# Masking a top-k attention row with its threshold as the bias

## The chip, the cores and the metric

The kernel runs on one core of a Trainium2 chip. The metric is the device time of one execution in microseconds. Five engines of the core work side by side, each through its own queue, in order: TensorE (PE in the profile; its weight loads are PEld), VectorE (DVE), ScalarE (ACT), GpSimd (POOL) and SyncE (SP), which issues most of the transfers here. An engine waits for another by semaphores.

## What is computed

Two blocks in a row: attention in which each query keeps only its 32 best keys, then a two-layer network with ELU between the layers. 8 batches, 8 heads, 576 positions, 64 per head; then 4608 tokens of 512, widened to 2048. Cut to what matters:

```python
scores = scale * np.matmul(q, k.transpose(0, 1, 3, 2))
kth = np.partition(scores, -32, axis=-1)[..., -32:-31]     # the threshold
scores = np.where(scores >= kth, scores, -1000000000.0)
scores = scores - np.max(scores, axis=-1, keepdims=True)
attn = np.exp(scores)
attn = attn / (np.sum(attn, axis=-1, keepdims=True) + 1e-09)
x = np.matmul(attn, v)            # then heads are put side by side: (4608, 512)
h = x @ w_in
g = np.where(h > 0.0, h, np.exp(np.minimum(h, 0.0)) - 1.0)
out = g @ w_out
```

## The kernel before

**Steps.** The attention is cut into 144 steps. A step is up to 128 queries of a pair of heads, so it has two score tiles of 128 queries by 576 keys, numbered i = 0 and 1. For each step these things happen, spread over several rounds of the main loop so that the engines overlap:

- `scores` (L299, L307): TensorE multiplies queries and keys, ScalarE copies the result out of PSUM into the tile `sc`. This runs two steps ahead.
- `select` (L341, L346, L353), or `select_row` in the first eight steps (L318, L322, L328): VectorE finds the 32 largest of each row, eight at a time. A maximum instruction gives the eight largest, a match-and-replace takes them out, and so on four times. The first eight stay in `u.first`, whose first column is the largest of the row. The last eight stay in `u.last`, whose eighth column is the threshold.
- `mask` (L366 to L370), once for each of the two tiles: two small GpSimd instructions form `neg` (minus the threshold) and `gap` (threshold minus largest), then two ScalarE activations over the whole tile, in place: a leaky ReLU with a slope of 1e30 on the negative side, and the exponential with the row sum as a second output. The first leaves the kept scores as score minus threshold and throws the others far below zero. The second adds `gap`, so that the kept ones become score minus largest, and the others give zero.
- `normalise` (L380 to L387): GpSimd forms the reciprocal of the row sums in small instructions and multiplies both tiles by it.
- `turn` (L406, L407): TensorE transposes the tile, ScalarE copies it to `et`.
- `attend` (L432, L459): TensorE multiplies with v, ScalarE copies the result to `xT`.

The network works on blocks of tokens as they become complete: `hidden` (L504 on TensorE; L514, L517 and L519 on ScalarE; the closing gate L476 on VectorE) and `project` (L529, L538). `feed` hands out these pieces between the attention's parts, paced by a list of due times.

**Weights.** The weights come in as 64-bit words and are turned into fp32 on the chip. Each of 32 pieces takes three ScalarE activations (L174, L175, L178), one GpSimd instruction (L179), one VectorE instruction (L186) and one more on GpSimd (L187). All ScalarE parts are issued from within `select_row` in the first eight steps, two pieces for each score tile, ahead of that tile's `mask`.

**Order.** From step 8 on (`tight`) the instructions of TensorE, ScalarE, VectorE and GpSimd stand in their queues as the program lists them. The opening lines and the first eight steps differ: the opening is in manual order too, but steps 0 to 7 are outside it, and the framework's planner, which walks through a model of the program by priority and readiness, decides the order in each queue. In these steps `mask` is called for the step in hand, right after the selection of each tile:

```python
                next(passes)
                mask(cur, i)
                feed(n, 0.25)
```

From step 8 on it is called one round later, for the step before: `mask(prev, 0)` after the first maxima of the step in hand, `mask(prev, 1)` two passes later, then `normalise(prev)` at the end of the round. Step 7 was already masked, and is skipped there.

The small tiles (`neg`, `gap`, `den`, the rows of eight) come from a pool with four buffers for each name.

Of the kernel before, what the change touches and what calls it, by code (L numbers as in the profile page):

```python
# [8 lines left out]
AF = mybir.ActivationFunctionType  # L9
ALU = mybir.AluOpType  # L10
FP32 = mybir.dt.float32
# [5 lines left out]
TOP_K = 32  # L17
TAKEN = -1.0e30
EPS = 1.0e-9
STEEP = 1.0e30  # L20
HIDDEN = {1: 1.1, 2: 1.85, 3: 2.7}
PROJECT = 3.55

# [58 lines left out]
def kernel(  # L82
# [9 lines left out]
    nc = tc.nc  # L92
    P = nc.NUM_PARTITIONS
# [12 lines left out]
    scale = 1.0 / float(D) ** 0.5  # L106
# [3 lines left out]
    def pool(name, bufs, **kw):  # L110
        return ctx.enter_context(tc.tile_pool(name=name, bufs=bufs, **kw))
# [7 lines left out]
    small = pool("small", 4)  # L119
# [161 lines left out]
    def turn_qk(whole=False):  # L281
        while turning:
            if next(turning[0], turning) is turning:
                turning.pop(0)
            elif not whole:
                return
# [3 lines left out]
    def scores(u):  # L290

        u.sc = scpool.tile([P, 2, S], FP32, tag="sc", name="sc")
        q0 = QUERIES + u.t.qt * P
        for half in range(2):
            for h, i, rows in u.heads:
                kq = kqT[u.t.b, h // 2]
                part = slice(i * D, (i + 1) * D)
                k0 = (KEYS if i == 0 else 0) + half * HS
                nc.tensor.matmul(  # L299
                    wide[i][rows, half, 0:HS],  # L300
                    kq[part, q0 : q0 + u.t.ql],
                    kq[part, k0 : k0 + HS],
                    start=True,
                    stop=True,
                )
        for i in range(2):
            nc.scalar.activation(  # L307
                u.sc[:, i, :].rearrange("p (a s) -> p a s", a=2),
                wide[i][:, :, 0:HS], AF.Copy, scale=scale,
            )  # L310

    def select_row(u, i):
        if i == 0:
            u.first = small.tile([P, 2, 8], FP32, tag="m1", name="m1")
            u.last = small.tile([P, 2, 8], FP32, tag="m4", name="m4")
        sc = u.sc[:, i, :]
        m = u.first[:, i, :]
        nc.vector.max(m, sc)  # L318
        wk = wkpool.tile([P, S], FP32, tag=f"wk{i}", name="wk")
        cur = sc  # L320
        for r in range(TOP_K // 8 - 1):
            nc.vector.match_replace(wk[:], m, cur, TAKEN)  # L322
            cur = wk[:]
            if r < TOP_K // 8 - 2:
                m = small.tile([P, 8], FP32, tag=f"m{i}", name="m")[:]
            else:
                m = u.last[:, i, :]
            nc.vector.max(m, cur)  # L328
            if r > 0:
                hook()  # L330
            if r != 1:
                yield
# [21 lines left out]
            hook()  # L354
            yield

    def mask(u, i):

        if u.masked:
            return  # L360
        if i == 0:
            u.den = small.tile([P, 2], FP32, tag="den", name="den")
        u.masked = i == 1
        sc, low, top = u.sc[:, i, :], u.last[:, i, 7:8], u.first[:, i, 0:1]
        neg = small.tile([P, 1], FP32, tag="neg", name="neg")
        nc.gpsimd.tensor_scalar_mul(neg[:], low, -1.0)  # L366
        gap = small.tile([P, 1], FP32, tag="gap", name="gap")
        nc.gpsimd.tensor_tensor(gap[:], low, top, ALU.subtract)
        nc.scalar.activation(sc, sc, AF.Prelu, bias=neg[:], alpha=STEEP)  # L369
        nc.scalar.activation(  # L370
            sc, sc, AF.Exp, bias=gap[:], accum_out=u.den[:, i : i + 1]
        )

    def normalise(u):

        if u.normal:
            return
        u.normal = True
        den = small.tile([P, 2], FP32, tag="dene", name="dene")
        nc.gpsimd.tensor_scalar_add(den[:], u.den[:], EPS)  # L380
        rec = small.tile([P, 2], FP32, tag="rec", name="rec")
        nc.gpsimd.tensor_tensor(rec[:], den[:], power[:], ALU.pow)
        nc.gpsimd.tensor_tensor(den[:], den[:], rec[:], ALU.mult)
        nc.gpsimd.tensor_scalar(den[:], den[:], -1.0, 2.0, ALU.mult, ALU.add)
        nc.gpsimd.tensor_tensor(rec[:], rec[:], den[:], ALU.mult)
        for i in range(2):
            nc.gpsimd.tensor_scalar(  # L387
                u.sc[:, i, :], u.sc[:, i, :], rec[:, i : i + 1], 1.0, ALU.mult, ALU.mult
            )
# [26 lines left out]
    def attend(g):  # L416
        t = g.tiles[0]
        ps = ps_t.tile([P, JP], FP32, tag="t", name="avps")
        n = P if t.rem else sum(x.ql for x in g.tiles)
        for k in range(2 if t.rem else 1):  # L420
            hp = 2 * g.hp + k if t.rem else g.hp
            vt = vT[t.b, hp]
            for c in range(J + 1):
                for i in range(2):
                    chunk = J if c == J else i * (J + 1) + c
                    w = g.et[:, chunk, :, :].rearrange("p a q -> p (a q)")
                    cols = slice(0, n)
                    if t.rem:
                        c0 = R * (k if i == 0 else 1 - k)
                        w = w[:, c0 : c0 + R]  # L430
                        cols = slice(k * R, (k + 1) * R)
                    nc.tensor.matmul(  # L432
                        ps[i * D : (i + 1) * D, cols],
                        vt[:, 2 * J + i if c == J else i * J + c, :],
                        w,
                        start=(c == 0),
                        stop=(c == J),
                    )
        if t.rem:
            finish(t.block, 2, slice(2 * g.hp, 2 * g.hp + 2), t.cols,  # L440
                   ps[:, 0:n].rearrange("p (a q) -> p a q", a=2))
            return
        c0 = 0
        tiles = list(g.tiles)
        while tiles:
            blk, lo, parts = tiles[0].block, tiles[0].cols.start, 0
            while tiles and tiles[0].block is blk:
                parts += 1
                hi = tiles.pop(0).cols.stop
            finish(blk, parts, g.hp, slice(lo, hi), ps[:, c0 : c0 + hi - lo])  # L450
            c0 += hi - lo
# [201 lines left out]
    def step(n):  # L653
        return steps[n] if 0 <= n < NS else None
# [3 lines left out]
    for n in range(NS + 3):  # L658
        for fn, args in todo.pop(n, []):
            fn(*args)  # L660
        ahead, cur, prev, done = step(n + 2), step(n), step(n - 1), step(n - 2)
        if n < tight:
            turn_qk(True)
            scores(ahead)
            for i in range(2):
                passes = select_row(cur, i)
                next(passes)
                if i == 0:
                    while closing:
                        attend(closing.pop(0))  # L670
                elif prev:
                    normalise(prev)
                    turn(prev, main)
                    turn(prev, rest)
                    turn(prev, other)
                feed(n, 0.25)
                next(passes)
                mask(cur, i)
                feed(n, 0.25)
            continue  # L680
        if n == tight:
            ctx.enter_context(tc.manual_schedule(engines=engines))
        passes = select(cur) if cur else iter(range(4))
        if ahead:
            scores(ahead)
        while closing:
            attend(closing.pop(0))
        next(passes)
        feed(n, 0.25)
        if prev:  # L690
            mask(prev, 0)
        turn_qk()
        next(passes)
        feed(n, 0.25)
        if done:
            turn(done, main)
            turn(done, rest)
        if prev:
            mask(prev, 1)
        next(passes)  # L700
        feed(n, 0.25)
        if done:
            turn(done, other)
        next(passes)
        if prev:
            normalise(prev)
        feed(n, 0.25)
        turn_qk(True)
# [36 lines left out]
```

## Time and profile before

| | |
|---|---|
| runs | 1666.01, 1667.40, 1667.79 us; median 1667.4 |
| profiled execution | 1667.02 us, its span 1665.2 us |
| instructions | 25986 |
| TensorE busy | 1592.8 us (96%) |
| VectorE busy | 1495.8 us (90%) |
| ScalarE busy | 1165.1 us (70%) |
| GpSimd busy | 630.5 us (38%) |
| granted TensorE clock, mean | 0.977 |

The span runs from the first to the last instruction of the profiled execution; 1.8 us of its time lie outside it. A line of the profile names the source line, the engine, the operation, the tiles written and read (out<-in) and their shapes. A group's line then gives the number of instructions, the busy time in us, the mean duration in ns, and the idle time of the engine just ahead of them with what ended it. A waits line gives total us, number of times and the longest. A timeline line starts with the start in us and the duration. The duration covers an instruction's whole record, and on VectorE and ScalarE records of neighbours overlap, so the next one can start before the printed end. The lines by stage give busy us and, in brackets, the number of instructions for each engine; then the granted clock, the share of the transfer engines in use, and GB/s.

### The profile page before, as it was taken

Reading aid. Unit: us, or ns where it says so; the run is one execution under the profiler, and the core shown is the slowest. Engines: PE = TensorE matmul, PEld = TensorE weight load, DVE = VectorE, ACT = ScalarE, POOL = GpSimd, SP = SyncE. Lnnn points to the kernel's source line nnn. Section 1 sums busy time; section 2 is a strip of 40 time slices with the busy share of each in tenths; the row PEclk is TensorE's granted clock in tenths of the full one; section 3 lists DMA queues with packets and bytes.
Section 4 is the critical chain, followed back from the end, with each engine's and each line's share of the span. In section 5 each row is a group of like instructions: output and inputs, shape, how many; then the busy total and the mean of one; then the engine's idle time right before and its main releaser. Section 6 shows DMA issues by size and latency. Waiting matters only on the chain.

```text
span 1665.2 us, 25986 instructions
## 1 busy us (share of the span) xinstructions
PE 1592.8 (96%) x8528; PEld 1031.5 (62%) x8528; DVE 1495.8 (90%) x3044; ACT 1165.1 (70%) x2377; POOL 630.5 (38%) x1719
## 2 busy tenths in 40 slices
PE   5589999999999999999999999999999999999999
PEld 3366677657574767656566676755557575755565
DVE  5887999999999999999999999999999999998500
ACT  6998777668686777678667685868758585857521
POOL 3775444333334334333334333333333343332200
PEclk9578999999999999999999999999999999999999
DMA  7540120001100110001100111001200100000000
GB/s 211 171 144 7 23 50 29 7 15 44 48 1 8 43 42 22 1 28 37 42 14 1 50 29 35 1 14 43 50 13 1 28 15 29 7 7 7 7 13 13
DMA packets 101126, 56.21 MB, mean 34 GB/s; under 512 B 84096, under 2 KB 92288, under 8 KB 100992
## 3 DMA queue, kind: packets, MB, share of 16 engines
q1 hardware_dynamic: 99792, 54.26, 11.7%
q8 instruction: 68, 1.11, 0.3%
q14 instruction: 66, 0.54, 0.1%
q10 hardware_dynamic: 1200, 0.30, 0.1%
HBM read 45.09 MB, written 9.44 MB: 33 GB/s over the span
## 4 chain that ended last, share of the span: by engine, by line
PE 65%; DVE 21%; ACT 9%; POOL 3%; issue 2%; SPq 0%; DMA 0%; ACTq 0%; POOLq 0%; DVEq 0%
PE ops L529 24%; PE hps L504 20%; DVE wk L346 9%; DVE m L353 8%; PE avps L432 7%; PE scps L299 6%; PE eps L406 5%; DVE m L341 3%; ACT sc L370 2%; ACT sc L369 1%; DVE gT L476 1%; ACT raw L175 1%; PE qkps L269 1%; ACT et L407 1%; POOL w_in L187 1%
## 5 line engine op out<-in xcount | busy, mean ns | idle before, releaser
L353 DVE MAX8 m<-wk 128x8 f32<-128x576 f32 x816 | 577.0, 750 | 0.0
L504 PE MATMUL hps<-xT,w_in 128*128 128x256 f32 (+2 forms) x2432 | 548.1, 374 | 12.5 <-ACT xT L459 12.3
L529 PE MATMUL ops<-w_out,gT 128*128 128x512 f32 x1152 | 522.8, 598 | 0.0
L504 PEld LDWEIGHTS hps<-xT,w_in 128*128 128x128 f32 x2432 | 406.5, 193 | 109.2 <-issue 23.8
L346 DVE MATCH_REPLACE8 wk<-m,wk 128x576 f32<-128x576 f32 x544 | 400.8, 746 | 0.0
L529 PEld LDWEIGHTS ops<-w_out,gT 128*128 128x128 f32 x1152 | 208.7, 190 | 233.0 <-issue 219.5
L380 POOL TENSOR_SCALAR dene<-den 128x2 f32<-128x2 f32 x144 | 35.9, 249 | 771.2 <-ACT sc L370 770.6
L369 ACT ACTIVATE sc<-sc,neg 128x576 f32<-128x576 f32 x288 | 226.8, 788 | 89.2 <-POOL neg L366 89.0
L370 ACT ACTIVATE sc<-sc,gap 128x576 f32<-128x576 f32 x288 | 224.1, 778 | 25.7 <-ACT sc L369 0.7
L387 POOL TENSOR_SCALAR sc<-sc,rec 128x576 f32<-128x576 f32 x288 | 221.0, 778 | 14.9
L307 ACT ACTIVATE sc<-scps 128x576 f32<-128x576 f32 x288 | 174.0, 659 | 73.3 <-PE scps L299 73.3
L299 PE MATMUL scps<-kqT 64*128 64x288 f32 (+1 forms) x1280 | 201.8, 440 | 21.2 <-ACT kqT L275 7.9
L407 ACT COPY et<-eps 128x512 f32<-128x512 f32 x288 | 166.8, 579 | 55.2 <-PE eps L406 55.0
L346 DVE MATCH_REPLACE8 wk<-m,sc 128x576 f32<-128x576 f32 x272 | 200.4, 746 | 0.0
L432 PE MATMUL avps<-et,vT 128*64 128x256 f32 (+2 forms) x2080 | 193.3, 326 | 4.8 <-ACT et L407 4.6
L406 PEld LDWEIGHTS eps<-ident,sc 128*128 128x128 f32 x1152 | 143.6, 144 | 83.8 <-issue 46.2
L476 DVE SCALAR_TENSOR_TENSOR gT<-n,gT 128x512 f32<-128x512 f32 (+1 forms) x132 | 100.2, 759 | 102.0 <-ACT n L519 101.9
L341 DVE MAX8 m<-sc 128x8 f32<-128x576 f32 x272 | 191.8, 748 | 0.0
L406 PE MATMUL eps<-ident,sc 128*128 128x128 f32 x1152 | 175.7, 278 | 15.4 <-POOL sc L387 13.0
L432 PEld LDWEIGHTS avps<-et,vT 128*64 128x64 f32 x2080 | 122.6, 141 | 79.1 <-issue 22.8
L299 PEld LDWEIGHTS scps<-kqT 64*128 64x128 f32 (+1 forms) x1280 | 108.1, 181 | 91.9 <-issue 44.2
L514 ACT ACTIVATE n<-hps 128x512 f32<-128x512 f32 (+1 forms) x156 | 88.0, 564 | 71.4 <-PE hps L504 67.5
(47 smaller groups left out, 1170.2 us busy)
## 6 DMA issues: line engine op xcount, KB each, us to landing
kin<-in_k_dram SPq DMA_DIRECT2D x64, 128.0 KB, 2.8
raw<-in_moe_w_in_dram SPq DMA_DIRECT2D x16, 512.0 KB, 5.4
vT<-in_v_dram SPq DMA_DIRECT2D x64, 128.0 KB, 2.3
raw<-in_moe_w_out_dram SPq DMA_DIRECT2D x16, 512.0 KB, 3.9
out_dram<-osb SPq DMA_DIRECT2D x32, 256.0 KB, 2.3
qin<-in_q_dram SPq DMA_DIRECT2D x62, 128.0 KB, 2.8
kin<-in_k_dram SPq DMA_DIRECT2D x32, 32.0 KB, 2.4
vT<-in_v_dram SPq DMA_DIRECT2D x64, 16.0 KB, 2.2
```

The source lines that it names most:

```text
L299: nc.tensor.matmul(wide[i][rows, half, 0:HS], kq[part, q0 : q0 + u.t.ql], kq[part, k0 : k0 + HS], start=True, stop=True,)
L341: nc.vector.max(found[i], cur[i])
L346: nc.vector.match_replace(wk[i], found[i], cur[i], TAKEN)
L353: nc.vector.max(found[i], cur[i])
L369: nc.scalar.activation(sc, sc, AF.Prelu, bias=neg[:], alpha=STEEP)
L370: nc.scalar.activation(sc, sc, AF.Exp, bias=gap[:], accum_out=u.den[:, i : i + 1])
L387: nc.gpsimd.tensor_scalar(u.sc[:, i, :], u.sc[:, i, :], rec[:, i : i + 1], 1.0, ALU.mult, ALU.mult)
L406: nc.tensor.transpose(ps[:, c * P : (c + 1) * P], sc[:, c0 : c0 + P], ident[:])
L407: nc.scalar.copy(g.et[:, chunks, u.at, :], ps[:, 0 : n * P].rearrange("p (c q) -> p c q", c=n),)
L432: nc.tensor.matmul(ps[i * D : (i + 1) * D, cols], vt[:, 2 * J + i if c == J else i * J + c, :], w, start=(c == 0), stop=(c == J),)
L504: nc.tensor.matmul(blk.h[:, f % bank, :], w_in[:, i, f * P : (f + 1) * P], blk.xT[:, i, 0:n_tok], start=(i == 0), stop=(i == NC - 1),)
L529: nc.tensor.matmul(blk.o[:], blk.gT[f // NG][:, f % NG, s * P : (s + 1) * P], w_out[:, f, :], start=(f == 0), stop=(f == NF - 1),)
```

## The change

The leaky ReLU is given the difference the other way round: threshold minus score, which it forms with a scale of -1 and the threshold itself as the bias. The scores below the threshold are then the positive ones and pass as they are; the kept ones are negative and are made small by a slope of 2 to the power -96. The exponential multiplies by minus 2 to the power 96, which brings the kept ones back to score minus threshold and throws the others far below zero, and adds `gap` as before. `neg` is not needed any more. The constant becomes a power of two. The engine that forms `gap` is now an argument of `mask`: GpSimd by default, VectorE where `mask` is called in the first eight steps.

```diff
-STEEP = 1.0e30
+STEEP = 2.0**96
...
-    def mask(u, i):
+    def mask(u, i, engine=nc.gpsimd):
...
         sc, low, top = u.sc[:, i, :], u.last[:, i, 7:8], u.first[:, i, 0:1]
-        neg = small.tile([P, 1], FP32, tag="neg", name="neg")
-        nc.gpsimd.tensor_scalar_mul(neg[:], low, -1.0)
         gap = small.tile([P, 1], FP32, tag="gap", name="gap")
-        nc.gpsimd.tensor_tensor(gap[:], low, top, ALU.subtract)
-        nc.scalar.activation(sc, sc, AF.Prelu, bias=neg[:], alpha=STEEP)
+        engine.tensor_tensor(gap[:], low, top, ALU.subtract)
+        nc.scalar.activation(sc, sc, AF.Prelu, scale=-1.0, bias=low, alpha=1.0 / STEEP)
         nc.scalar.activation(
-            sc, sc, AF.Exp, bias=gap[:], accum_out=u.den[:, i : i + 1]
+            sc, sc, AF.Exp, scale=-STEEP, bias=gap[:], accum_out=u.den[:, i : i + 1]
         )
...
-                mask(cur, i)
+                mask(cur, i, nc.vector)
```

## The prediction

> **What bounds the kernel now.** I read the page first (VectorE 90% busy, TensorE 96%), then the busy time of each engine by stage, because shares over the whole span mix stages with different limits.
>
> ```profile
> core 0: us, PE busy (x) PEld busy (x) DVE busy (x) ACT busy (x) POOL busy (x), PEclk, DMA share, GB/s
> ...
> 36.00:58.00 22.00, 6.46 (x43) 4.93 (x43) 15.02 (x31) 21.27 (x34) 13.26 (x24) 0.65 0.59 203
> 58.00:139.00 81.00, 63.22 (x320) 46.88 (x320) 59.74 (x122) 79.72 (x139) 58.50 (x98) 0.67 0.42 129
> ...
> 146.00:850.00 704.00, 688.16 (x4018) 453.97 (x4017) 704.00 (x1441) 506.01 (x1060) 275.54 (x793) 1.00 0.10 27
> 850.00:1550.00 700.00, 697.55 (x3670) 444.40 (x3669) 668.93 (x1355) 496.19 (x1030) 258.46 (x739) 1.00 0.07 20
> 1550.00:1606.00 56.00, 55.75 (x187) 27.46 (x186) 15.66 (x32) 18.36 (x39) 10.36 (x29) 1.00 0.04 10
> ```
>
> The reader is to see three limits, one after the other. From 36 to about 145 us (steps 0 to 7, with the weight conversion) ScalarE is full: 21.27 + 79.72 of 103 us, so 2.0 us are idle. From 146 to 850 VectorE is busy in all 704 us. From 850 to the end TensorE is: 697.55 of 700. A microsecond saved counts only where it lies on the full engine of its stage.
>
> Next I read the groups with shapes kept apart, for the masking instructions and for two that show what an immediate costs.
>
> ```profile
> L369 ACT ACTIVATE sc<-sc,neg 128x576 f32<-128x576 f32 x288 | 226.8, 788 | 89.2 <-POOL neg L366 89.0
> L370 ACT ACTIVATE sc<-sc,gap 128x576 f32<-128x576 f32 x288 | 224.1, 778 | 25.7 <-ACT sc L369 0.7
> ...
> L366 POOL TENSOR_SCALAR neg<-m 128x1 f32<-128x1 f32 x288 | 74.1, 257 | 74.3 <-DVE m L353 63.1 <-DVE m L328 10.7
> ...
> L514 ACT ACTIVATE n<-hps 128x512 f32<-128x512 f32 x108 | 64.5, 597 | 43.8 <-PE hps L504 42.5
> L517 ACT ACTIVATE gT<-hps 128x512 f32<-128x512 f32 x108 | 64.5, 597 | 0.0
> ...
> L368 POOL TENSOR_TENSOR gap<-m,m 128x1 f32<-128x1 f32 x288 | 56.0, 194 | 0.1
> ```
>
> The tempting number is the 89.0 us that ScalarE sat idle until `neg` was there. The view of the waits, cut by stage, says where: 60.0 us (39 times) between 146 and 850, 25.7 (32 times) between 850 and 1550, 3.3 (once) after that; together 89.0. None is left for the first 146 us. What ScalarE waited for between 36 and 146 us is only this:
>
> ```profile
> ACT et L407 <- PE eps L406: 2.0, 3, 0.7
> ACT et L407 <- PE scps L406: 0.2, 1, 0.2
> ```
>
> The timeline of GpSimd ahead of one of those three waits, then ScalarE's own:
>
> ```profile
> 64.43 0.21 POOL L366 TENSOR_SCALAR neg<-m 128x1 f32<-128x1 f32 x1 [2.41 <-DVE m L328]
> 64.60 0.19 POOL L368 TENSOR_TENSOR gap<-m,m 128x1 f32<-128x1 f32 x1
> 64.88 1.61 POOL L179 TENSOR_SCALAR raw<-raw 128x512 f32<-128x512 f32 x2
> 66.57 2.30 POOL L187 TENSOR_TENSOR w_in<-raw 128x512 int32<-128x512 int32 x2
> 68.96 0.23 POOL L380 TENSOR_SCALAR dene<-den 128x2 f32<-128x2 f32 x1
> ...
> 70.92 1.48 POOL L387 TENSOR_SCALAR sc<-sc,rec 128x576 f32<-128x576 f32 x2
> ```
>
> ```profile
> 71.42 0.80 ACT L369 ACTIVATE sc<-sc,neg 128x576 f32<-128x576 f32 x1
> 72.88 0.58 ACT L407 COPY et<-eps 128x512 f32<-128x512 f32 x1 [0.65 <-PE eps L406]
> ```
>
> GpSimd works in order: `neg` held it for 2.41 us, with weight conversion and normalisation queued behind. ScalarE later waits 0.65 us for a transpose that waited for that normalisation.
>
> **`neg` goes (288 instructions on GpSimd).** In steps 8 to 143 the first activation is released by VectorE's maximum directly. Worked on one step: the maximum's record ends near 503.7 us, `neg` starts at 503.76, the activation at 504.02, so about 0.26 us sooner. At most 72 waits of 0.26 us = 19 us of ScalarE idleness go; the rest of the 89 us is waiting for VectorE itself. Up to 850 us VectorE has no idle time to give back: 0. What was late next is VectorE's maximum. From 850 on TensorE would have to wait for ScalarE to gain, and its whole idle time there is 2.4 us, put down mostly to scores copies and transposed keys, not to masks: I take 0, bounds -2.4 and 0. If these covers were gone, 19 us would be the price. Where GpSimd was behind with a normalisation (near 153 us, a wait of 2.48 us), the first activation starts early but the second still needs `gap` from the same queue.
>
> **`gap` on VectorE (16 instructions, steps 0 to 7).** No such VectorE instruction is in the trace. The nearest small one is the value load of 128x8 (L346, mean 82 ns; the next instruction starts 0.07 us after it): 16 x 0.07 = 1.1 us. The Trainium skill, page "VectorE: DVE Perf Modes", section "Side-by-side: where the cycles go for N=2048 bf16", gives every instruction some 150 cycles of start-up at 0.96 GHz, an estimate of 0.16 us, or 16 x 0.16 = 2.5 us. I take the trace's 1.1 us and keep 2.5 as the end. Either is covered between 36 and 139 us, where VectorE is busy 74.76 of 103 us (28 us idle). Only three masks fall into 16 to 36 us, where VectorE is nearly full: 0.2 to 0.5 us, were they on the path. Below zero is excluded on VectorE itself. `gap` waits for nothing there, both inputs being VectorE's own, except a free buffer (four): at the sixteenth mask that means the exponential of the twelfth, which ended at 112.1 us, 11 us before `gap` can start. Behind it in VectorE's queue stand selection and conversion.
>
> **GpSimd relieved (32 instructions in steps 0 to 7).** 16 x (0.26 + 0.19) = 7.2 us less, and no stop at `neg`. At 64 us: the first L178 ends at 63.77, so L179 could start at 63.85, 1.03 us before 64.88. L187 and normalisation follow about 1 us sooner, the transpose with them, and the 0.65 us wait goes. The other two waits (0.70 at 57.2 us, 0.63 at 87.2) have the same queue ahead of them. Sum 0.70 + 0.65 + 0.63 = 2.0 us on the engine that is full to 146 us. A rule speaks against part of it: "GPSIMD Engine Reference", section "Specifications", says that GpSimd contends with VectorE instructions that have two SBUF inputs, and `gap` has two. The trace shows that contention: a `neg` at 504.43 us took 0.57 us beside the two-input L476, against a median of 220 ns. By the rule up to 16 x 0.16 = 2.5 us return to GpSimd of 7.2 taken off; by the trace's duration 1.1. The 1 us lead at each wait survives both.
>
> **The turned signs.** L514 (scale -1) and L517 (none) both take 597 ns, so a scale as an immediate costs nothing. Both activations keep one bias column. A bias read from the eighth column of a row, instead of from a tile of its own, has no row of its own; I take 0. As a bound, L369's mean and median differ by 7 ns (788, 781), and 16 masks of that are 0.1 us, either sign.
>
> **The sum.** 2.0 saved, 0 in the steady steps, 0 for VectorE. Against the profiled execution (span 1665.2, time 1667.02): 1665.0. The median of the runs is 0.4 above: 1665.4.
>
> **The rivals.** Steps 0 to 7 are not in the manual order; the framework places their instructions, and the trace shows that it does move them: step 8's first maximum (L341) ran at 120.56 us, before step 7's L328 at 122.54.
>
> *A new order at the start.* ScalarE was idle from 24.3 to 26.69 us, and the first threshold was there at 25.96 (a maximum's record of 0.75 us from 25.21), but the two L369 of step 0 stand behind two L307 and one L275, at 28.23. With no `neg` to wait for they may be placed first. Then they start near 26.0 and the chain mask, normalisation, transpose, conversion comes 2.0 us sooner. The delayed L307 are not needed until VectorE's L318 at 35.84. For it: an idle engine. Against: the placed order may stay as it was. Time: 1665.4 - 2.0 = 1663.4.
>
> *A worse order at the hand-over.* VectorE's steady run begins at 139.14 us, after a gate (L476, 138.53) that waited 3.42 us for the exponential L519. On ScalarE that L519 (137.69) stands just ahead of a pair of conversions; such a pair takes 4.65 us (66.91 to 71.56). If the removal and the added VectorE instruction let the planner place one more pair ahead of L519, everything after starts 4.65 us later. The 2.0 us hang on the same order, so I count them as lost with it: 1667.4 + 4.65 = 1672.0 (1670.0 if they survive). One displaced pair decides it. For it: the planner sees other ready times. Against: ScalarE was 19 us behind `neg` at the sixteenth mask (123.39 to 142.73), so `neg` did not decide its order. The mirror case, a pair moved behind, gives 1660.8, with the first rival 1658.8.
>
> *It does nothing.* The three waits close for another reason: 1667.4.
>
> **How the numbers follow.** About 0.2% (3.3 us) is what a measurement of this kernel tells from no change: faster means below 1664.1, slower above 1670.7. The forecast, with the case of nothing, 0.50; the better orders 0.31, all but 0.01 beyond the bound; a worse one 0.19, of which 0.02 for the milder 1670.0, so 0.17 beyond the bound. That gives faster 0.30, same 0.53, slower 0.17. The range 1659 to 1672 reaches to the mirror case and to one pair lost.
>
> **What would show it.** L366 is gone, and 16 small VectorE instructions appear. Waits of ScalarE for L366 turn into waits for VectorE's maxima. The first L346 starts near 137 us instead of 139.14. VectorE stays full for the 700 us after it and TensorE to the end, both stages as long as before. The forecast is wrong if the steady stages change their length, if the start moves by over 4 us, or if ScalarE gets idle time in the first 145 us.

## The result and the profile after

| | before | after |
|---|---|---|
| median of the runs | 1667.59 us (20 runs, 1665.69 to 1669.1) | 1664.1 us (20 runs, 1663.01 to 1665.44) |
| profiled execution, its span | 1667.02, 1665.2 us | 1665.44, 1663.6 us |
| GpSimd busy | 630.5 us | 570.3 us |
| VectorE busy | 1495.8 us | 1498.0 us |

The ratio is 0.9981, with a 95% interval of 0.9975 to 0.9987. That is 3.2 us less, between 2.2 and 4.2: a small gain, but a real one. (The two medians themselves lie 3.5 us apart.) The forecast was 1665.4, 2.0 us below the median of 1667.4 that it started from. The profiled execution of the changed kernel is the highest of its 20 runs, so the difference of the two spans, 1.6 us, is too small a reading of the gain; why it came out so high is told under before_again.

The busy time by stage of the changed kernel, with the columns and the stages as in the prediction:

```profile
36.00:58.00 22.00, 6.99 (x43) 5.09 (x42) 15.53 (x35) 20.82 (x34) 11.66 (x17) 0.66 0.53 188
58.00:139.00 81.00, 64.23 (x332) 47.97 (x332) 63.61 (x136) 81.00 (x141) 55.60 (x78) 0.67 0.42 133
...
146.00:850.00 704.00, 688.44 (x4019) 455.01 (x4018) 704.00 (x1440) 507.43 (x1063) 248.41 (x654) 1.00 0.10 27
850.00:1550.00 700.00, 697.55 (x3671) 444.31 (x3670) 668.39 (x1357) 494.63 (x1029) 231.59 (x609) 1.00 0.07 20
```

ScalarE is now busy in all 81.00 us from 58 to 139, where 1.28 us were idle before. From 36 to 58 it is idle for 1.18 us, where it was 0.73. The other two limits stand: VectorE 704.00 of 704, TensorE 697.55 of 700. GpSimd has lost 27 us in each of these two stages, and no other engine there moved by as much as 2 us.

The groups that mask, with shapes kept apart (busy us, mean ns; then the idle time ahead of them and what ended it):

```profile
L372 ACT ACTIVATE sc<-sc,m 128x576 f32<-128x576 f32 x288 | 228.2, 793 | 48.9 <-DVE m L353 48.7
L373 ACT ACTIVATE sc<-sc,gap 128x576 f32<-128x576 f32 x288 | 225.0, 781 | 38.5 <-POOL gap L371 15.2 <-ACT sc L372 0.4
...
L371 POOL TENSOR_TENSOR gap<-m,m 128x1 f32<-128x1 f32 x272 | 56.1, 221 | 91.2 <-DVE m L353 91.2
...
L371 DVE TENSOR_TENSOR gap<-m,m 128x1 f32<-128x1 f32 x16 | 5.0, 312 | 0.0
```

`neg` is gone. The leaky ReLU is released by VectorE's maximum itself, and the exponential waits 15.2 us for `gap`, which is now the first GpSimd instruction behind that maximum. ScalarE's idle time ahead of the two activations was 89.2 + 25.7 = 114.9 us and is 48.9 + 38.5 = 87.4: 27.5 us are gone. The kernel gained 3.2. Nearly all of these 27.5 lay beside full engines, as the prediction had it. What ScalarE still waits for between 36 and 146 us, from the view of the waits:

```profile
ACT sc L307 <- PE scps L299: 0.9, 1, 0.9
ACT et L410 <- PE scps L409: 0.2, 1, 0.2
```

The three waits for transposed tiles (0.70, 0.65, 0.63) are gone; one for scores is new. The place shown in the prediction, on the timelines of GpSimd and of ScalarE in the changed kernel:

```profile
64.47 1.61 POOL L179 TENSOR_SCALAR raw<-raw 128x512 f32<-128x512 f32 x2 [2.44 <-ACT raw L178]
66.16 1.04 POOL L187 TENSOR_TENSOR w_in<-raw 128x512 int32<-128x512 int32 x1
...
68.68 0.22 POOL L383 TENSOR_SCALAR dene<-den 128x2 f32<-128x2 f32 x1
...
70.63 1.48 POOL L390 TENSOR_SCALAR sc<-sc,rec 128x576 f32<-128x576 f32 x2
```

```profile
63.63 1.29 ACT L178 ACTIVATE raw<-raw 128x512 f32<-128x512 f32 x2
...
71.94 0.82 ACT L372 ACTIVATE sc<-sc,m 128x576 f32<-128x576 f32 x1
72.60 0.63 ACT L410 COPY et<-eps 128x512 f32<-128x512 f32 x1
```

GpSimd's stop is now ended by L178, not by a maximum. The first L178 ends at 63.63 + 0.65 = 64.28 and L179 starts at 64.47, 0.19 us behind it; before it was 1.11 us behind. (The row of two L178 is 1.29 us long; one takes 0.65.) So the lead gained is 0.92 us (1.03 forecast), and the copy L410 carries no bracket any more: it waits for nothing.

### The profile page after: what moved, and what is told of

The parts are those of the page before. It is cut to its first block, busy times and chain, and to the rows that moved or that the text cites. A ratio compares the mean times of both kernels' runs of the same rounds, so it can differ in the third digit from the quotient of the medians.

```text
span 1663.6 us, 25707 instructions
## 1 busy us (share of the span) xinstructions
PE 1592.8 (96%) x8528; PEld 1032.3 (62%) x8528; DVE 1498.0 (90%) x3060; ACT 1163.5 (70%) x2377; POOL 570.3 (34%) x1415
## 3 DMA queue, kind: packets, MB, share of 16 engines
q8 instruction: 68, 1.11, 0.3%
## 4 chain that ended last, share of the span: by engine, by line
PE 57%; DVE 32%; ACT 7%; issue 2%; POOL 1%; SPq 0%; DMA 0%; ACTq 0%; DVEq 0%; POOLq 0%
PE ops L532 21%; PE hps L507 18%; DVE wk L346 14%; DVE m L353 12%; PE avps L435 6%; PE scps L299 6%; PE eps L409 4%; DVE m L341 4%; DVE gT L479 2%; ACT raw L175 2%; ACT sc L373 1%; PE qkps L269 1%; ACT sc L372 1%; ACT raw L174 1%; ACT raw L178 1%
## 5 line engine op out<-in xcount | busy, mean ns | idle before, releaser
L346 DVE MATCH_REPLACE8 wk<-m,wk 128x576 f32<-128x576 f32 x544 | 398.7, 738 | 0.0
L372 ACT ACTIVATE sc<-sc,m 128x576 f32<-128x576 f32 x288 | 228.2, 793 | 48.9 <-DVE m L353 48.7
L373 ACT ACTIVATE sc<-sc,gap 128x576 f32<-128x576 f32 x288 | 225.0, 781 | 38.5 <-POOL gap L371 15.2
L410 ACT COPY et<-eps 128x512 f32<-128x512 f32 x288 | 167.6, 582 | 66.8 <-PE eps L409 66.6
L346 DVE MATCH_REPLACE8 wk<-m,sc 128x576 f32<-128x576 f32 x272 | 199.3, 738 | 0.0
```

The source lines that it names most:

```text
L346: nc.vector.match_replace(wk[i], found[i], cur[i], TAKEN)
L372: nc.scalar.activation(sc, sc, AF.Prelu, scale=-1.0, bias=low, alpha=1.0 / STEEP)
L373: nc.scalar.activation(sc, sc, AF.Exp, scale=-STEEP, bias=gap[:], accum_out=u.den[:, i : i + 1])
```

## One table for all kernels

Each trace can be cut at two instants that all kernels have. The first is the start of the fourth activation of L174 (at 36.67 us before), where ScalarE's full stretch with the weight conversion begins. The second is the start of the first L346 of step 8, where VectorE's full stretch begins. "Start" is the time up to the first, "conversion" the time from the first to the second, "steady" the rest of the span. "Behind L175" is the part of the conversion behind the start of the tenth L175 (at 54.16 us before). From there to the second instant ScalarE has the same instructions in the same order in all kernels; ahead of it the last four rows differ. These four times come from the profiled execution; median, range and ratio to before come from the timed runs (7 to 20 of each kernel, 5 or 6 where a star stands). Each ratio is to runs of before that were taken along with the kernel, with medians of 1667.42 to 1667.59.

| kernel | start | conversion | behind L175 | steady | median (range) | ratio [95%] |
|---|---|---|---|---|---|---|
| before | 36.67 | 102.48 | 84.98 | 1526.10 | 1667.59 (1665.69 to 1669.1) | 1 |
| before_again | 35.36 | 102.47 | 84.99 | 1526.09 | 1667.16 (1665.71 to 1669.02) | 0.9997 [0.9988, 1.0006] |
| after | 36.95 | 101.26 | 82.85 | 1525.43 | 1664.1 (1663.01 to 1665.44) | 0.9981 [0.9975, 0.9987] |
| again_after | 35.77 | 100.91 | 82.78 | 1525.21 | 1664.61 (1662.99 to 1665.62) | 0.998 [0.9972, 0.9989] |
| new_early | 36.94 | 101.02 | 83.55 | 1526.68 | 1665.8 (1664.55 to 1666.41) | 0.9987 [0.9978, 0.9995] |
| new_late | 37.07 | 103.78 | 85.38 | 1525.16 | 1666.43 (1664.99 to 1668.21) | 0.9994 [0.9985, 1.0003] |
| gap_gpsimd | 35.75 | 102.37 | 84.49 | 1525.46 | 1665.37 (1663.82 to 1666.99) | 0.9988 [0.998, 0.9997] |
| idle_neg | 36.09 | 100.79 | 82.71 | 1525.38 | 1664.05 (1663.28 to 1664.96) | 0.9978 [0.9969, 0.9987] |
| no_gap_late | 35.94 | 100.87 | 82.70 | 1524.38 | 1662.89 (1662.19 to 1664.32) | 0.9972 [0.9961, 0.9983] |
| gap_vector_all* | 37.79 | 101.06 | 82.74 | 1534.62 | 1674.83 (1672.71 to 1675.29) | 1.0039 [1.0027, 1.0052] |
| old_vector_early | 35.30 | 102.30 | 83.27 | 1526.32 | 1664.37 (1663.74 to 1665.7) | 0.9981 [0.9972, 0.999] |
| mix | 35.24 | 102.40 | 83.38 | 1525.39 | 1663.98 (1662.71 to 1664.85) | 0.9978 [0.9969, 0.9987] |
| mix_no_gap* | 34.81 | 102.30 | 83.26 | 1524.27 | 1663.21 (1661.88 to 1663.73) | 0.9971 [0.9959, 0.9982] |
| no_gap_all* | 35.40 | 100.52 | 82.25 | 1524.24 | 1662.76 (1661.94 to 1663.83) | 0.9971 [0.9959, 0.9982] |

Two things are to be read from it. "Start" scatters by over 1 us between executions of one program, while "conversion" and "steady" of one program repeat to 0.01 us (before) or 0.35 and 0.22 us (after). And "steady" falls into groups. The six kernels that turn the signs from step 8 on and form `gap` on GpSimd there have 1525.16 to 1525.46; the four with the old masking there have 1526.09 to 1526.68. The groups stand apart, but a difference of 0.5 us within a group is no effect: new_early, whose steps from 8 on are those of before, has 1526.68.

## The experiments

**before_again: how far two executions of one program differ.** No edit.

> The kernel before against itself: ratio 1.000, within 0.5 us. For the second profile: the stretch from the first L346 to the end repeats to 0.3 us (1526.1), while the first L346 may lie anywhere from 138 to 141 us, since new_late, whose start is the same program, had 140.85. If instead the stretch moves by more than 0.5 us, the 0.9 us read from it for the steps after 8 is not safe.

Conversion and steady stretch came out equal to 0.01 us, but the start was 1.31 us shorter. The difference is there at 24 us. One row of TensorE's timeline, of before and then of before_again:

```profile
24.37 2.29 PE L299 MATMUL scps<-kqT 64*128 64x288 f32 x8 [0.75 <-ACT kqT L265]
```

```profile
24.21 1.24 PE L299 MATMUL scps<-kqT 64*128 64x288 f32 x8 [0.75 <-ACT kqT L265]
```

The same eight matmuls took 2.29 us in one execution and 1.24 in the other, with a granted clock of 1.00 in both from 24 to 27 us; why, no run here shows. The profile of after drew the long start too: 36.95, and a clock of 0.50 from 34 to 38 us, where before had 0.77 and before_again 0.98. With 1.18 us less of it, as in again_after, it would lie near the middle of its runs instead of at their top.

**again_after: the changed kernel once more.** No edit.

> The changed kernel once more, for a second profile. Theory A (the gain is GpSimd's relief in the first eight steps, passed on by a full ScalarE): the first L346 starts 1 to 2.5 us before the 139.14 us of before (the first profile of the changed kernel had 138.21, with the granted TensorE clock at 0.50 between 34 and 38 us where before had 0.77), and the time is 2 to 4 us below before. Theory B (the gain is made after step 8, by the 288 waits that lose neg): the hand-over differs by under 1 us and the rest of the gain grows between 146 and 1600 us. Theory C (fewer GpSimd instructions beside VectorE's two-input gate L479): the gates in 146 to 850 us lose up to 1.4 us of extra time against before.

The median was 1664.61. Conversion and steady stretch were short again: 1.57 and 0.89 us below before, against 1.22 and 0.67 in the first profile. The steady stretch was forecast to stay as it was, and did not.

**new_early and new_late: each half of the change alone.** In the first, steps 0 to 7 have the new masking and the later ones the old, with the edit below. In the second it is the other way round: its condition reads `if engine is nc.vector:`.

```diff
     def mask(u, i, engine=nc.gpsimd):
...
+        if engine is nc.gpsimd:
+            neg = small.tile([P, 1], FP32, tag="neg", name="neg")
+            nc.gpsimd.tensor_scalar_mul(neg[:], low, -1.0)
...
+            nc.scalar.activation(sc, sc, AF.Prelu, bias=neg[:], alpha=STEEP)
...
+            return
```

> Turned subtraction and gap on VectorE in steps 0 to 7 only; from step 8 on neg, gap and the old subtraction as before. Theory A: the whole gain, 2 to 3.5 us below before. Theory B: at most 1 us below before. Theory C: as A for its part before 146 us, so 1 to 2 us below before.

> The old masking in steps 0 to 7, the turned one (gap on GpSimd) from step 8 on. Theory A: no change, within 0.7 us of before. Theory B: nearly the whole gain, 2 to 3.5 us below before. Theory C: 0.3 to 1.4 us below before, with the gates in 146 to 850 us shorter by that much.

The table takes the halves apart. new_early has the short conversion (101.02) and the old steady stretch (1526.68). new_late has the short steady stretch (1525.16), and its conversion is not short (103.78). It is even 1.3 us longer than before, through a wait of 0.89 us for scores and one of 0.32 for a transposed tile that before did not have. Its instructions in these steps are those of before, so this is scatter: its granted clock was 0.50 from 34 to 38 us, as in the profile of after, which has the same wait for scores. By the medians new_early is 1.6 us under before and new_late 1.0; the interval of new_late includes no change. So the change gains in two places, where the prediction had one.

**gap_gpsimd: is it the move of `gap` to VectorE, or the turned signs, that clears the start?**

```diff
-                mask(cur, i, nc.vector)
+                mask(cur, i)
```

> The changed kernel with gap on GpSimd in the first eight steps too, so neg alone is gone there and gap still waits for VectorE in GpSimd's queue. Theory A, where the stop at VectorE's maximum counts: gap takes over neg's stop (2.41 us before the one at 64.43 us), only 16 x 0.26 us of work go, and half the gain or less is left, 0.5 to 1.5 us below before. If only the number of GpSimd instructions counted: two thirds of the gain, about 2.3 us. Theory B: the same time as the changed kernel.

The conversion is back at 102.37. GpSimd's timeline of this kernel, then ScalarE's:

```profile
63.53 0.19 POOL L371 TENSOR_TENSOR gap<-m,m 128x1 f32<-128x1 f32 x1 [2.40 <-DVE m L328]
```

```profile
57.21 0.59 ACT L410 COPY et<-eps 128x512 f32<-128x512 f32 x1 [0.53 <-PE eps L409]
...
71.80 0.59 ACT L410 COPY et<-eps 128x512 f32<-128x512 f32 x1 [0.26 <-PE eps L409]
```

`gap` has taken over the stop of `neg` (2.40 us, after 2.41), and the waits at 57 and 72 us are back, shorter than before (0.70 and 0.65); one of 0.68 us at 101 us is new. Taking one of two small instructions away only passes the stop to the other. At the start, the move of `gap` is what pays. The median was 2.05 us under before, more than the 0.5 to 1.5 expected, and near the 2.3 of the rival that counts instructions. But 0.6 of it is the shorter steady stretch, which the expectation left out, so it is the waits that decide here and not the median.

**idle_neg: why does the steady stretch get shorter?** One theory was that ScalarE's masks start sooner, since they no longer wait for GpSimd; its rival was that GpSimd has fewer instructions. The edit gives GpSimd an instruction like `neg` back, which nothing waits for.

```diff
+        if engine is nc.gpsimd:
+            idle = small.tile([P, 1], FP32, tag="idle", name="idle")
+            nc.gpsimd.tensor_scalar_mul(idle[:], low, -1.0)
         gap = small.tile([P, 1], FP32, tag="gap", name="gap")
```

> The changed kernel, but from step 8 on GpSimd still forms minus the threshold ahead of gap, into a tile that nothing reads, so its work is as before while ScalarE's first activation no longer waits for it. ScalarE's and TensorE's queues are the same. Steps 0 to 7 are as in the changed kernel. Theory B (what counts after step 8 is that ScalarE starts a mask earlier): the stretch from the first L346 to the end is 1525.2 to 1525.5 us as with the turned masking, and the time about 2.8 us below before. Theory C (what counts is 272 fewer GpSimd instructions beside VectorE's gates): the stretch is 1526.1 to 1526.7 us as with neg, and the time 1.6 us below before.

The steady stretch stayed short, 1525.38, although the groups of this kernel show the work in place:

```profile
L372 POOL TENSOR_SCALAR idle<-m 128x1 f32<-128x1 f32 x272 | 71.7, 264 | 82.7 <-DVE m L353 82.7
```

The number of instructions on GpSimd is not it. What counts is when ScalarE begins.

How can an earlier ScalarE shorten a stretch in which VectorE has no idle time? The instructions of VectorE must have become shorter, and the one that did is the closing gate, which has two inputs in SBUF and collides with GpSimd's instructions over whole tiles. One gate of a step near 790 us, on the timelines of GpSimd and VectorE before:

```profile
791.25 1.47 POOL L387 TENSOR_SCALAR sc<-sc,rec 128x576 f32<-128x576 f32 x2
792.16 1.37 DVE L476 SCALAR_TENSOR_TENSOR gT<-n,gT 128x768 f32<-128x768 f32 x1
792.70 0.92 POOL L366 TENSOR_SCALAR neg<-m 128x1 f32<-128x1 f32 x1
```

and the same gate in again_after:

```profile
787.93 1.48 POOL L390 TENSOR_SCALAR sc<-sc,rec 128x576 f32<-128x576 f32 x2
...
789.37 0.34 POOL L371 TENSOR_TENSOR gap<-m,m 128x1 f32<-128x1 f32 x2
789.64 0.94 DVE L479 SCALAR_TENSOR_TENSOR gT<-n,gT 128x768 f32<-128x768 f32 x1
```

Before, the normalisation was still running (to 792.72) when the gate began, and the gate took 1.37 us. With masks that start sooner, the normalisation was over (789.41) before the gate began at 789.64, and the gate took 0.94. This gate repeats: 1.37 us in before_again and 1.39 in new_early, with the old masking in this step, and 0.93 in after, idle_neg and new_late.

The sum of such lengths is less safe. VectorE's busy time in gates (and their number) by stage, in before and then in before_again:

```profile
146.00:850.00 704.00, 41.84 (x56) 1.00 0.10 27
850.00:1550.00 700.00, 49.10 (x63) 1.00 0.07 20
```

```profile
146.00:850.00 704.00, 40.69 (x56) 1.00 0.10 27
850.00:1550.00 700.00, 49.10 (x63) 1.00 0.07 20
```

and in idle_neg:

```profile
146.00:850.00 704.00, 40.59 (x56) 1.00 0.10 27
850.00:1550.00 700.00, 48.26 (x63) 1.00 0.07 20
```

Up to 850 us the 40.59 of idle_neg tells nothing, since one program has 41.84 in one profile and 40.69 in the next. From 850 on, both profiles have 49.10, and idle_neg has 48.26. What repeats throughout is the time from a gate's start to the start of VectorE's next instruction, with idle time taken off. From the first L346 of step 8 on, VectorE's queue holds the same 2849 instructions in the same order in all kernels of the next table, so they can be paired one by one. The table shows by how much a kernel's first L346 of a step stands earlier (minus) or later than before's, both counted from the first L346 of step 8. Its last two columns show how much less or more all gates take by this measure, the 56 up to step 78 and the 71 behind it (36.58 and 49.81 us before):

| step | 40 | 58 | 78 | 83 | 98 | end | gates to 78 | gates behind |
|---|---|---|---|---|---|---|---|---|
| before_again | 0.02 | -0.01 | -0.01 | -0.01 | -0.01 | -0.01 | -0.03 | 0.00 |
| new_early | 0.78 | 0.49 | 0.51 | 0.50 | 0.51 | 0.58 | 0.52 | 0.04 |
| new_late | 0.31 | -0.38 | -0.56 | -1.23 | -1.24 | -0.94 | -0.56 | -0.87 |
| after | 0.66 | -0.04 | -0.25 | -0.93 | -0.94 | -0.67 | -0.28 | -0.80 |
| again_after | 0.32 | -0.33 | -0.51 | -1.19 | -1.19 | -0.89 | -0.52 | -0.79 |
| idle_neg | 0.49 | -0.11 | -0.31 | -0.98 | -0.99 | -0.72 | -0.37 | -0.88 |
| no_gap_late | 0.99 | 0.14 | 0.00 | -1.59 | -1.74 | -1.72 | -0.03 | -1.58 |

Up to step 78, at 852 us, the gates are the whole difference: their column is that of step 78 to within 0.06 us. The masks alone are worth 0.56 us there between before and new_late, and some 0.8 between new_early and after or idle_neg, whose first eight steps are the same program. It is not a smooth gain. Up to step 40 all kernels but before_again have even lost time, new_early with the old masking too, so the turned signs are not all of that loss. Then after, again_after, idle_neg and new_late gain some 1.5 us by step 98, and give back 0.3 by the end. Behind step 78 their gates save 0.8 to 0.9 us and the stretch only 0.4, because VectorE waits some 0.5 us longer ahead of later gates.

The largest single piece, 0.68 us, falls between steps 78 and 83. Of it 0.30 is a gate again, at 877.64 us of before (0.89 us from start to start there, 0.59 in again_after). The rest lies at a gate near 865 us that waits for ScalarE's exponential. Before, again_after and no_gap_late, each from VectorE's timeline:

```profile
866.78 0.69 DVE L476 SCALAR_TENSOR_TENSOR gT<-n,gT 128x512 f32<-128x512 f32 x1 [2.12 <-ACT n L519]
```

```profile
863.45 0.69 DVE L479 SCALAR_TENSOR_TENSOR gT<-n,gT 128x512 f32<-128x512 f32 x1 [1.74 <-ACT n L522]
```

```profile
863.12 0.69 DVE L482 SCALAR_TENSOR_TENSOR gT<-n,gT 128x512 f32<-128x512 f32 x1 [0.79 <-ACT n L525]
```

At this one place past the stretch where VectorE is full, ScalarE sets the pace, and what it saves counts: 0.38 us of the 0.68.

**no_gap_late: `gap` taken away from step 8 on.** The exponential then has no bias column there; the shift by the largest score is left out in these steps.

```diff
+        shift = 0.0
+        if engine is nc.vector:
...
+            shift = gap[:]
         nc.scalar.activation(
-            sc, sc, AF.Exp, scale=-STEEP, bias=gap[:], accum_out=u.den[:, i : i + 1]
+            sc, sc, AF.Exp, scale=-STEEP, bias=shift, accum_out=u.den[:, i : i + 1]
```

> The changed kernel, but from step 8 on without gap: the exponential takes no shift by the largest score (the normalisation divides it out again but for the 1e-9), so GpSimd has no mask work there and no exponential waits for it. Queues of the other engines as in the changed kernel. Theory B: ScalarE loses its 15.2 us of waits for gap (23 times), most of them where VectorE or TensorE is full, so 0 to 0.7 us below the changed kernel. Theory C: another 272 instructions less, so about 1 us below the changed kernel, with the gates' extra time in 146 to 850 us (0.87 us in its second profile) near 0.

The steady stretch fell by a further 1.0 us (1524.38 against 1525.38 of idle_neg), mostly at the gate just shown, whose wait fell from 1.74 to 0.79. Theory B had allowed 0.7 us for it, theory C had about 1; but C looked for the gain in the gates up to 850 us, and up to step 78 they take as long as before (-0.03 in the table). The run does not tell cleanly whether the earlier start of the exponential did that, because another thing changed with it, in the group of the exponential:

```profile
L376 ACT ACTIVATE sc<-sc 128x576 f32<-128x576 f32 x272 | 185.9, 684 | 8.7
```

Without the bias column it takes 684 ns, not the 781 of the changed kernel.

**gap_vector_all: what a small VectorE instruction costs where nothing covers it.**

```diff
-    def mask(u, i, engine=nc.gpsimd):
+    def mask(u, i, engine=nc.vector):
```

> The changed kernel with gap on VectorE in all steps, where VectorE is full to 850 us: what such an instruction costs where nothing covers it. By the spacing in the changed kernel's trace (the next instruction starts 0.06 us after a gap that meets no GpSimd work): some 140 of them up to step 78 make 8.4 us, and later ones up to 2.4 us more per 20 steps against VectorE's 3 us of idleness per 10 steps, so 6 to 12 us above the changed kernel. By the 150 cycles of start-up of the Trainium skill's page VectorE: DVE Perf Modes (0.16 us): 140 x 0.16 = 22 us or more above it.

It is slower than before: 1.0039 [1.0027, 1.0052], and 10.2 us above again_after by the medians. From the first L346 to that of step 60, VectorE took 537.09 us against 529.39 in again_after, with 103 more instructions: 7.7 us, or 0.075 us each. On its VectorE timeline:

```profile
303.84 0.14 DVE L371 TENSOR_TENSOR gap<-m,m 128x1 f32<-128x1 f32 x1
303.89 0.08 DVE L346 MATCH_VALUE_LOAD wk<-m,sc 128x8 f32 x1
```

The record is 0.14 us long, but the next one starts 0.05 us after it. The 0.07 us that the prediction took from the value load were right, and the estimate of 0.16 us from the Trainium skill ("VectorE: DVE Perf Modes", section "Side-by-side: where the cycles go for N=2048 bf16") is twice too high here. Moving `gap` pays only where VectorE has room: in steps 0 to 7.

**old_vector_early: the move alone, with the old signs.** `neg` and `gap` both on VectorE in steps 0 to 7, nothing else changed.

```diff
-    def mask(u, i):
+    def mask(u, i, engine=nc.gpsimd):
...
-        nc.gpsimd.tensor_scalar_mul(neg[:], low, -1.0)
+        engine.tensor_scalar_mul(neg[:], low, -1.0)
...
-        nc.gpsimd.tensor_tensor(gap[:], low, top, ALU.subtract)
+        engine.tensor_tensor(gap[:], low, top, ALU.subtract)
...
-                mask(cur, i)
+                mask(cur, i, nc.vector)
```

> The old subtraction everywhere, but in steps 0 to 7 both neg and gap on VectorE, so GpSimd is relieved there as in the changed kernel without the turned sign. Theory A (the start gains by GpSimd's relief): 1 to 2 us below before, like new_early (1.6), with the first L346 near 137 to 138 us. If the turned sign itself were needed at the start: no change from before. The planner places five TensorE runs and a few ScalarE instructions of the start differently here, which can add a us either way.

1664.37, as fast as the whole change by the medians, and 3.2 us under before where 1 to 2 were expected; the steady stretch is as before (1526.32). So the early gain doesn't need the turned signs. In the table the time seems saved in "start" and not in "conversion" (102.30), but the placed order on ScalarE and TensorE differs from before in this kernel, so the first instant is not the same point of the work. The tenth L175 is: behind it this kernel takes 83.27 us, where before takes 84.98 and after 82.85. The three waits for transposed tiles are gone here too, and one of 0.42 us at 100 us has come. So the relief takes the same path.

**mix, mix_no_gap and no_gap_all: do the parts add?** mix has the old signs on VectorE in steps 0 to 7 and the turned signs later. mix_no_gap is mix without `gap` from step 8 on. no_gap_all is the changed kernel without `gap` in any step. The last two leave out the shift by the largest score where there is no `gap`. What mix adds to old_vector_early (mix_no_gap has neither the `gap` nor the bias in it):

```diff
...
+        if engine is nc.gpsimd:
+            engine.tensor_tensor(gap[:], low, top, ALU.subtract)
+            nc.scalar.activation(sc, sc, AF.Prelu, scale=-1.0, bias=low, alpha=2.0**-96)
+            nc.scalar.activation(
+                sc, sc, AF.Exp, scale=-(2.0**96), bias=gap[:],
+                accum_out=u.den[:, i : i + 1],
+            )
+            return
...
```

What no_gap_all takes from the changed kernel:

```diff
-        gap = small.tile([P, 1], FP32, tag="gap", name="gap")
-        engine.tensor_tensor(gap[:], low, top, ALU.subtract)
...
-            sc, sc, AF.Exp, scale=-STEEP, bias=gap[:], accum_out=u.den[:, i : i + 1]
+            sc, sc, AF.Exp, scale=-STEEP, accum_out=u.den[:, i : i + 1]
```

> The start of old_vector_early (old subtraction, neg and gap on VectorE in steps 0 to 7; 3.2 us below before) and the turned masking with gap on GpSimd from step 8 on (0.95 us by the stretch). If the two parts add: 4.1 us below before, about 1663.3, and 0.8 us below the changed kernel. If the start's better order was an accident of those runs: as the changed kernel, 1664.1 to 1664.6.

> The start of old_vector_early and, from step 8 on, the turned masking without gap (no shift by the largest score there). If the parts add: another 1.0 us below mix, 5 us below before, about 1662.3, with the stretch at 1524.4 us.

> The changed kernel without gap in all steps. From step 8 on as no_gap_late (stretch 1524.4 us). In the first eight the exponential waits for its own engine alone, and the planner orders ScalarE and TensorE anew there: if the order is harmless, 1662.9 like no_gap_late; a better or worse order shows as a first L346 more than 1 us off 136.8, and moves the time by as much.

In the steady stretch the parts do what they did alone: 1525.39 for mix (-0.7), 1524.27 and 1524.24 without `gap` (-1.8). In the times they don't separate. mix is 0.4 us below old_vector_early by the medians where I expected 1.1, its interval overlaps that of the changed kernel, and mix_no_gap is 0.8 below mix for 1.0 expected. no_gap_all has the lowest median, 1662.76, some 1.3 us below the changed kernel; its interval (0.9959 to 0.9982) overlaps that of the changed kernel, so that it beats it is likely and not shown.

## Why the prediction came out nearly right

- **The limits by stage: right.** 27.5 us of ScalarE's idleness ahead of the masks went, for at most 19 us forecast, and at most 0.9 of them reached the end, by way of the gates.
- **The three waits: right in place, mechanism and size, but another wait came.** Behind the tenth L175 ScalarE was idle for 1.98 us before. That is 0.00 in after, again_after, idle_neg, no_gap_late and gap_vector_all, and this part is 2.1 to 2.3 us shorter. But these five have a wait of 0.6 to 0.9 us for scores ahead of it, and new_early, which has none, has one of 0.75 for a transposed tile at 100 us. The whole conversion got shorter by only 1.2 to 1.7 us in these six, the kernels with both the turned signs and `gap` on VectorE at the start. The sum named no wait that would be next in line there. The change does not make the wait for scores by itself: new_late has it with the old masking.
- **"Up to 850 us VectorE has no idle time to give back: 0": the step that failed.** The idle time was indeed zero, but the lengths of VectorE's instructions were not fixed. I had even shown a `neg` lengthened beside the two-input gate, and did not turn the case round: the gate is lengthened too, and when GpSimd's large instruction moves, that changes. The measured term is -0.25 to -0.5 us in the changed kernel. "The steady stages change their length" was one of the prediction's own signs of being wrong, and it came.
- **From 850 on, 0 between bounds of -2.4 and 0: inside the bounds.** The measured term is -0.4. The wait at 865 us fell by 0.38 us. It lies past 850, where I had looked at TensorE alone; a VectorE still waiting for ScalarE just after the hand-over was not in the sum.
- **The turned signs: right.** The two activations took 793 and 781 ns on average, for 788 and 778 before; 16 times both differences is 0.1 us.
- **`gap` on VectorE: the price on the path right (none), the duration wrong.** Undisturbed they cost 0.06 to 0.07 us from one start to the next, but all 16 together took 3.96 us, not 1.1. Five of them took 0.52 to 0.92 us beside long GpSimd instructions. VectorE's idle time covered it.
- **The rivals fell.** ScalarE's and TensorE's queues hold the same instructions in the same order before and after; neither a better nor a worse order came about. VectorE's first L346 began at 138.21 and 136.69 us in the two profiles, for 137 forecast; but before_again had 137.84, so this sign tells little.

The parts that are shown add up to some 1.5 us at the start and 0.8 later, 2.3 in all. That this is so near the forecast of 2.0 is luck in part: the new wait and the gates, both missing from the sum, nearly cancel. The runs say 3.2, between 2.2 and 4.2. Part of what is between them is in which starts are compared. The wait for scores, in new_late and then in after, with a granted clock of 0.50 from 34 to 38 us in both; and the wait at 100 us in new_early:

```profile
38.64 0.65 ACT L307 ACTIVATE sc<-scps 128x576 f32<-128x576 f32 x1 [0.89 <-PE scps L299]
```

```profile
38.56 0.65 ACT L307 ACTIVATE sc<-scps 128x576 f32<-128x576 f32 x1 [0.94 <-PE scps L299]
```

```profile
100.90 0.59 ACT L420 COPY et<-eps 128x512 f32<-128x512 f32 x1 [0.75 <-PE eps L419]
```

Between these two kernels that both wait for scores, old masking against new, the conversion differs by 103.78 - 101.26 = 2.5 us. Between before and new_early, neither of which waits there, it differs by 102.48 - 101.02 = 1.5. With 0.7 to 0.9 for the steady stretch, that is an estimate of 2.2 to 3.4 us for the whole change, and the 3.2 of the runs lies in it. Which kind of start the timed runs had, their times don't tell, so the rest isn't settled. Nothing in the profiles says that the change shortens the stretch up to 36 us as well: "start" is 35.8 to 37.8 us in the six kernels above, and 35.4 to 37.1 in the three that have the old masking there in the old order.

## What to carry to other kernels

A small instruction on a queue that others stand in costs the stop that it makes there, not its 0.2 us; look for what is queued behind it, and remember that taking away one of two passes the stop to the other. "This engine is full, so nothing changes here" holds only while its instructions keep their lengths: where two engines lengthen each other, moving work on the idle one changes the full one. Before reading half a microsecond out of two profiles, cut them at common instants and profile the same program twice, so that scatter at the start isn't taken for an effect; and count an instruction from its start to the next one's, since the lengths of records added up to 1.15 us more in one of two profiles of the same program.

## What was unexpected in the hardware

Two-input instructions of VectorE and GpSimd's instructions hold each other up for long, measured by their own durations. The Trainium skill names the rule ("GPSIMD Engine Reference", section "Specifications"), and these traces give the price. From one start to the next, a gate 512 wide normally takes 590 ns, and up to 1051 in a collision; 768 wide, 857 and 1307. The `neg` beside the gate at 792.16 us took 0.92 us, for a median of 0.22. Even `gap`, one element wide, can be held by a long GpSimd instruction; VectorE's timeline of the changed kernel, then GpSimd's at that time:

```profile
110.87 1.00 DVE L371 TENSOR_TENSOR gap<-m,m 128x1 f32<-128x1 f32 x1
111.79 0.75 DVE L328 MAX8 m<-wk 128x8 f32<-128x576 f32 x1
```

```profile
110.58 2.27 POOL L187 TENSOR_TENSOR w_out<-raw 128x512 int32<-128x512 int32 x2
```

The next maximum started 0.92 us after `gap`, where it is 0.06 without a neighbour. Not every neighbour holds it: at 56.44 us `gap` took 0.07 us beside a normalisation that had begun 0.01 us ahead of it; why, no run here shows.

An exponential over 128x576 took 781 ns with a bias column and 684 with a constant: 0.1 us for the column. The Trainium skill ("ScalarE: Activation LUTs", section "What ACT_TABLE_LOAD costs") gives about 93 ns for such an operand, and these runs agree.
